# Linear attention and a SwiGLU FFN on one core: inputs laid out as (head half, 64 chunks of 9 tokens), and the work ordered anew

## The chip, the cores and the metric

One core of a Trainium2 chip. The metric is the device time of one execution in microseconds; the medians below are of two to seven executions. The span of a profile (first to last instruction) is 1.7 to 2.2 us shorter than the time of that execution. TensorE's granted clock is given where it matters. Engines: PE is TensorE, PEld its weight loads, DVE VectorE, ACT ScalarE, POOL GpSimd, SP SyncE, SPq SyncE's queue of DMA issues.

## The reference

```python
# q, k, v: (batch 8, heads 8, seq 576, head_dim 64), float32
def phi(x):
    return np.where(x > 0, x, np.exp(x) - 1.0) + 1.0
q_p, k_p = (phi(q), phi(k))
kv  = np.einsum('bhsd,bhse->bhde', k_p, v)
z   = np.sum(k_p, axis=2)
num = np.einsum('bhsd,bhde->bhse', q_p, kv)
den = np.einsum('bhsd,bhd->bhs', q_p, z)[..., None] + 1e-06
x   = (num / den)                       # -> (4608 tokens, 512)
g   = x @ w_gate                        # 512 x 1536
out = (g * sigmoid(g) * (x @ w_val)) @ w_out    # 1536 x 512
```

## The kernel before

A batch is 576 tokens. A group is 512 tokens through the FFN (12 blocks `l1`, then 4 tiles `l2`); nine groups make the 4608 tokens. The kernel before puts tokens in the partitions: 512 of a batch as 128 partitions of 4 tokens (rows of 1 KB per head), and the last 64 of two batches together as a tail tile (rows of 256 B). All tails make the ninth group. q, k and v come by one hardware queue, SyncE's; the weights by GpSimd's, which casts them to fp16 (9.44 MB of float32; its queue, q0 on the page, shows 4.72 MB). The order of issue is the program's order on each engine.

```python
def load(b, src, main, tail):
    nc.sync.dma_start(out=main[b % 2][:, :, :],
        in_=src[b][:, 0:NM, :].rearrange("h (p j) d -> p h (j d)", j=J))       # J = 4, NM = 512
    if b % 2 == 0:
        for e in range(2):
            nc.sync.dma_start(out=tail[(b // 2) % 2][TL * e:TL * e + TL, :, :], # TL = 64
                              in_=src[b + e][:, NM:S, :].rearrange("h p d -> p h d"))

def vcast(b, js):                    # ScalarE
    for j in js:
        nc.scalar.activation(out=vm[b % 2][:, j, :, 0:D], in_=v32[b % 2][:, :, D * j:D * j + D], func=AF.Copy, ...)

def mm1(b, half):                    # kv: per head pair 4 + 1 matmuls of 128 rows
    ...

for g in range(B + 1):
    ...                              # [cut: which step of batch g+1 or g+2 runs in which slot]
    for fb in range(FB):             # FB = 12
        if fb == 0 and g >= 0:
            if g + 2 < B:
                load_k(g + 2); load_q(g + 2); load_v(g + 2)
        l1(g, fb)                    # 8 matmuls, SiLU on ScalarE, product on VectorE
        run(ch[fb])                  # a step of batch g+1's attention
        ...
        if 4 <= fb < 8 and b2 < B:   # b2 = g + 2
            vcast(b2, [fb - 4])
    for t in range(4):
        l2(g, t)
        run(pa[t])                   # exp and phi of batch g+2
```

## Time and profile before

| | before |
|---|---|
| time, median (range) | 431.9 us (430.93 to 432.88) |
| span | 429.3 us |
| first matmul of the FFN | 34.9 us |
| group 0 / 1 / 2 / 3 / 4 / 5 | 76.7 / 41.7 / 45.5 / 39.1 / 46.1 / 40.4 us |
| group 6 / 7 / 8 | 36.7 / 32.0 / 31.2 us |
| after the last matmul | 4.8 us |

A group's length is the distance from its first gate matmul to that of the next, read from the timeline. The last group has nothing beside the FFN: 144 matmuls, about 0.216 us apart, make 31.2 us, so nine groups make 281 us of the span. Whatever else takes time must show as a group longer than 31.2 us or as time before the first group.

What was read first is the page's head (busy us, share of the span, count of instructions), its row of DMA queues, and for forty slices of 10.7 us the busy tenths of the DMA engines (one digit a slice) and the GB/s:

```profile
PE 332.6 (77%) x1672; PEld 154.6 (36%) x1672; DVE 240.4 (56%) x430; ACT 168.9 (39%) x271; POOL 10.5 (2%) x26
...
DMA  8899992001630069004701780046002002002004
GB/s 234 184 247 247 240 273 43 1 0 50 214 128 2 1 211 253 2 0 148 246 2 43 205 219 0 0 158 234 0 20 82 2 0 99 0 2 98 0 2 98
...
q1 hardware_dynamic: 40720, 37.75, 30.4%
```

For the first six slices the DMA engines are busy for 8 or 9 tenths of the time. The row q1 (packets, MB, share of the time of 16 engines): 0.304 x 429.3 x 16 = 2088 us of engine time for 37.75 MB.

The waits view (who, for whom: us in total, times, longest) names ScalarE waiting for v, and the timeline of ScalarE shows the longest case:

```profile
ACT vm_87 L168 <- DMA v_0_67<-in_v_dram: 42.5, 4, 22.7
...
ACT vm_88 L168 <- DMA v_1_68<-in_v_dram: 8.5, 2, 4.4
```

```profile
44.05 0.60 ACT L290 ACTIVATE sil_122<-pG_133 128x512 f16<-128x512 f32 x1 [1.13 <-PE pG_133 L287]
67.30 0.63 ACT L168 ACTIVATE vm_87<-v_0_67 128x512 f16<-128x512 f32 x1 [22.66 <-DMA v_0_67<-in_v_dram]
67.84 0.58 ACT L290 ACTIVATE sil_123<-pG_134 128x512 f16<-128x512 f32 x1
```

ScalarE runs in order. In block 4 of group 0 it reaches the v cast of batch 2, whose load is far back in the queue, and stands for 22.66 us (the bracket: idle time, and what ended it). The SiLU behind it waits too: its gate matmuls were issued by 45.36 us, and it starts at 67.84. TensorE waits with it: the next gate matmul comes at 68.47 us, after 20.14 us idle. The windows view (the stretch and its length; busy us of PE, PEld, DVE, ACT and POOL, with the number of instructions; then granted clock, DMA share, GB/s) of that stretch, under one of the first loads:

```profile
2.00:16.40 14.40, 2.97 (x20) 1.99 (x20) 6.03 (x15) 5.40 (x10) 2.17 (x9) 1.00 1.08 272
40.00:67.00 27.00, 8.33 (x39) 3.66 (x38) 2.57 (x4) 1.79 (x3) 0.00 (x0) 0.70 1.14 247
```

TensorE does 8.33 us of work in 27, at a clock of 0.70, while the DMA engines are full at 247 GB/s.

### The profile page before, as it was taken

What the parts mean: (1) busy time and instruction counts of PE and PEld (TensorE: products, weight loads), DVE (VectorE), ACT (ScalarE), POOL (GpSimd) and SP (SyncE); (2) the same over time, 40 slices, a digit from 0 to 9 for tenths busy, and PEclk for the clock granted to TensorE, in tenths of its full rate; (3) what the DMA queues carried; (4) which work ended last, traced back from release to release, by engine and by line L of the source; (5) the groups of instructions that cost most, each with busy time, mean ns of one, the idle gap of its engine ahead of it and who ended that gap; (6) DMA issues with size and microseconds to landing.
All of it is one profiled execution on the core that took longest, in us unless ns stands there. A gap on an engine that the chain in (4) does not pass through costs nothing.

```text
span 429.3 us, 4508 instructions
## 1 busy us (share of the span) xinstructions
PE 332.6 (77%) x1672; PEld 154.6 (36%) x1672; DVE 240.4 (56%) x430; ACT 168.9 (39%) x271; POOL 10.5 (2%) x26
## 2 busy tenths in 40 slices
PE   0329506386788995699879948998799999999995
PEld 0113202142334452245334523453345444444442
DVE  3583102467978663678576626786666772342431
ACT  3604006752344741564346513744365221321320
POOL 3420000000000000000000000000000000000000
PEclk9999856888899999799999996999899999999999
DMA  8899992001630069004701780046002002002004
GB/s 234 184 247 247 240 273 43 1 0 50 214 128 2 1 211 253 2 0 148 246 2 43 205 219 0 0 158 234 0 20 82 2 0 99 0 2 98 0 2 98
DMA packets 45494, 42.76 MB, mean 100 GB/s; under 512 B 13728, under 2 KB 42912, under 8 KB 45472
## 3 DMA queue, kind: packets, MB, share of 16 engines
q1 hardware_dynamic: 40720, 37.75, 30.4%
q0 software_dynamic: 4752, 4.72, 6.5%
q8 instruction: 13, 0.21, 0.2%
q14 instruction: 9, 0.07, 0.1%
HBM read 37.75 MB, written 9.44 MB: 110 GB/s over the span
## 4 chain that ended last, share of the span: by engine, by line
PE 52%; DMA 16%; SPq 15%; DVE 9%; ACT 4%; issue 3%; DVEq 0%; POOL 0%; ACTq 0%; POOLq 0%
PE pO_137 L297 11%; PE pO_138 L297 10%; SPq L102 10%; DMA v_0_67<-in_v_dram 7%; PE pG_133 L287 7%; PE pG_134 L287 7%; PE pV_135 L287 7%; PE pV_136 L287 6%; DMA v_1_68<-in_v_dram 5%; SPq L97 5%; DMA q_0_65<-in_q_dram 2%; DVE qp_81 L231 2%; DVE qp_82 L231 2%; DMA k_1_64<-in_k_dram 1%; DVE hT_121 L291 1%
## 5 line engine op out<-in xcount | busy, mean ns | idle before, releaser
L287 PEld LDWEIGHTS <-wg 128*128 128x128 f16 x432 | 42.5, 101 | 86.1 <-issue 43.9
L287 PEld LDWEIGHTS <-wv 128*128 128x128 f16 x432 | 43.5, 101 | 55.1 <-issue 7.3
L291 DVE SCALAR_TENSOR_TENSOR hT_120<-pV_136,sil_123 128x512 f16<-128x512 f32 x30 | 20.7, 689 | 61.3 <-ACT sil_123 L290 48.1
L290 ACT ACTIVATE sil_122<-pG_133 128x512 f16<-128x512 f32 x54 | 32.2, 597 | 53.2 <-PE pG_133 L287 53.1
L290 ACT ACTIVATE sil_123<-pG_134 128x512 f16<-128x512 f32 x54 | 32.1, 595 | 41.2 <-PE pG_134 L287 38.8
L287 PE MATMUL pG_134<-xT_0_112,wg 128*128 128x512 f16 x30 | 12.2, 408 | 32.9 <-ACT sil_123 L290 32.9
L291 DVE SCALAR_TENSOR_TENSOR hT_120<-pV_135,sil_122 128x512 f16<-128x512 f32 x30 | 20.7, 689 | 24.7 <-PE pV_135 L287 20.5
L297 PEld LDWEIGHTS <-hT_120 128*128 128x128 f16 x240 | 23.7, 100 | 28.4 <-issue 2.3
L303 ACT ACTIVATE osb_125<-pO_138 128x512 f32<-128x512 f32 x9 | 5.4, 597 | 65.9 <-PE pO_138 L297 65.9
L297 PE MATMUL pO_137<-wo,hT_120 128*128 128x512 f16 x120 | 29.2, 396 | 0.0
L291 DVE SCALAR_TENSOR_TENSOR hT_121<-pV_136,sil_123 128x512 f16<-128x512 f32 x24 | 16.5, 689 | 22.1 <-ACT sil_123 L290 11.6
L297 PE MATMUL pO_138<-wo,hT_120 128*128 128x512 f16 x120 | 27.5, 379 | 0.0
L297 PEld LDWEIGHTS <-hT_121 128*128 128x128 f16 x192 | 18.8, 98 | 22.6
L168 ACT ACTIVATE vm_87<-v_0_67 128x512 f16<-128x512 f32 x16 | 9.7, 625 | 42.5 <-DMA v_0_67<-in_v_dram 42.5
L291 DVE SCALAR_TENSOR_TENSOR hT_121<-pV_135,sil_122 128x512 f16<-128x512 f32 x24 | 16.5, 689 | 17.2 <-PE pV_135 L287 15.2
L297 PE MATMUL pO_137<-wo,hT_121 128*128 128x512 f16 x96 | 22.0, 379 | 0.0
L297 PE MATMUL pO_138<-wo,hT_121 128*128 128x512 f16 x96 | 22.0, 379 | 0.0
L221 DVE TENSOR_REDUCE den<-prod 128x16 f32<-128x1024 f16 x16 | 19.4, 1211 | 0.1
L301 DVE TENSOR_SCALAR osb_124<-pO_137 128x512 f32<-128x512 f32 x9 | 6.2, 691 | 17.9 <-PE pO_137 L297 17.9
L186 PE MATMUL pA_139<-vm_87,kp_79 128*128 128x129 f16 x32 | 4.6, 251 | 14.4 <-DVE kp_79 L133 13.7
L168 ACT ACTIVATE vm_88<-v_1_68 128x512 f16<-128x512 f32 x16 | 9.7, 625 | 8.5 <-DMA v_1_68<-in_v_dram 8.5
L252 PE MATMUL pA_139<-id_130,qp_81 128*128 128x128 f16 x32 | 3.8, 254 | 11.4 <-DVE qp_81 L231 11.3
(207 smaller groups left out, 663.2 us busy)
## 6 DMA issues: line engine op xcount, KB each, us to landing
k_0_63<-in_k_dram SPq DMA_DIRECT2D x4, 1024.0 KB, 6.8
v_0_67<-in_v_dram SPq DMA_DIRECT2D x4, 1024.0 KB, 9.6
q_0_65<-in_q_dram SPq DMA_DIRECT2D x4, 1024.0 KB, 9.9
k_1_64<-in_k_dram SPq DMA_DIRECT2D x4, 1024.0 KB, 7.2
q_1_66<-in_q_dram SPq DMA_DIRECT2D x4, 1024.0 KB, 9.6
v_1_68<-in_v_dram SPq DMA_DIRECT2D x4, 1024.0 KB, 11.4
out_dram<-osb_124 SPq DMA_DIRECT2D x8, 512.0 KB, 2.7
out_dram<-osb_125 SPq DMA_DIRECT2D x8, 512.0 KB, 3.3
```

What stands on the lines that cost most here:

```text
L97: nc.sync.dma_start(out=main[b % 2][:, :, :], in_=src[b][:, 0:NM, :].rearrange("h (p j) d -> p h (j d)", j=J))
L102: nc.sync.dma_start(out=tail[(b // 2) % 2][TL * e:TL * e + TL, :, :], in_=src[b + e][:, NM:S, :].rearrange("h p d -> p h d"))
L168: nc.scalar.activation(out=vm[b % 2][:, j, :, 0:D], in_=v32[b % 2][:, :, D * j:D * j + D], func=AF.Copy, bias=0.0, scale=1.0)
L186: nc.tensor.matmul(out=o, lhsT=kp[b % 2][:, j, P * hp:P * hp + P], rhs=vm[b % 2][:, j, :, :].rearrange("p h c -> p (h c)")[:, 130 * hp:130 ...
L221: nc.vector.tensor_reduce(out=den[:, cs], in_=prod[:, :, :].rearrange("p j (h d) -> p (j h) d", h=H), axis=AX.X, op=ALU.add)
L231: nc.vector.tensor_tensor(out=qv, in0=qv, in1=rden[:, H * j:H * j + H].unsqueeze(2).to_broadcast([P, H, D]), op=ALU.mult)
L287: nc.tensor.matmul(out=ps[:, :], lhsT=w[:, cc, P * fb:P * fb + P], rhs=xT[cc][g % 2][:, :], start=(cc == 0), stop=(cc == NH2 - 1))
L290: nc.scalar.activation(out=s[:, :], in_=pG[i][:, :], func=AF.Silu, bias=0.0, scale=1.0)
L291: nc.vector.scalar_tensor_tensor(out=hT[g % 2][:, fb, :], in0=pV[i][:, :], scalar=SC, in1=s[:, :], op0=ALU.mult, op1=ALU.mult)
L297: nc.tensor.matmul(out=ps[:, :], lhsT=hT[g % 2][:, fb, P * t:P * t + P], rhs=wo[:, fb, :], start=(fb == 0), stop=(fb == FB - 1))
L301: nc.vector.tensor_scalar(out=o[:, t % 2, :], in0=ps[:, :], scalar1=1.0 / SC, scalar2=None, op0=ALU.mult)
L303: nc.scalar.activation(out=o[:, t % 2, :], in_=ps[:, :], func=AF.Copy, bias=0.0, scale=1.0 / SC)
```

## The change

Its intent: no tail tiles, so every batch is handled alike, with 72 units of 64 tokens that are packed eight to a group; longer rows in the loads; and a better order at the start. Partitions are now (half of the heads, 64 chunks of 9 tokens). The kv product contracts over 64 rows, for two head halves in two row tiles of the array. Cut to its core:

```diff
-    def load(b, src, main, tail):
-        nc.sync.dma_start(out=main[b % 2][:, :, :],
-            in_=src[b][:, 0:NM, :].rearrange("h (p j) d -> p h (j d)", j=J))
-        ... (tails, cut)
+    def load(src, dst, b, lp):          # C = 64, J = 9
+        v4 = src[b].rearrange("(a l) (c j) d -> a c l (j d)", a=2, j=J)
+        for hh in range(2):
+            nc.sync.dma_start(out=dst[b % 2][C * hh:C * hh + C, 2 * lp:2 * lp + 2, :],
+                          in_=v4[hh][:, 2 * lp:2 * lp + 2, :])
...
+    def mm1(b, lp):
+        ...
+        for j in range(J):
+            for hh in range(2):
+                rows = slice(C * hh, C * hh + C)
+                nc.tensor.matmul(out=kvb[b][hh][:, 256 * lp:256 * lp + W],
+                    lhsT=kp[b % 2][rows, j, P * lp:P * lp + P],
+                    rhs=vm[b % 2][rows, j, :, :]...[:, 130 * lp:130 * lp + W],
+                    start=(j == 0), stop=(j == J - 1))
...
+    ld_k(0)
+    ld_q(0)
     ...                                                              # [cut: constants]
+    ld_v(0)
+    nc.gpsimd.tensor_copy(out=gate[:, 0:1], in_=v32[0][:, 3, 0:1])   # GpSimd waits for v
+    ld_w1(0)                              # first third of the gate and value weights
+    sp_after(wv[0:1, 0, 0:1], 2)          # SyncE waits for it
+    ld_k(1)
+    ld_q(1)
+    ld_w1(1)
+    ld_w1(2)
+    ... (second layer's weights, cut)
+    sp_after(wv[0:1, 0, DF - 512:DF - 511], 1)
+    ld_v(1)
...
-            if 4 <= fb < 8 and b2 < B:
-                vcast(b2, [fb - 4])
+        if g >= 1 and b2 < B:             # none in group 0
+            ...
+            sl[8] = sl[8] + [lambda: vcast(b2, 0)]
+            sl[9] = sl[9] + [lambda: vcast(b2, 1)]
+            if fb == 4 and b2 < B:
+                ld_k(b2)
+                ld_q(b2)
+                ld_v(b2)
```

Also in it, and cut here: batches 0, 1 and 2 take z directly from phi(k) by 64x64-tiled matmuls, so that q need not wait for v; the first four blocks of groups 0 and 1 use tanh for the sigmoid, which spares ScalarE a change of its table between exp and the FFN's activation; the second layer borrows the first layer's PSUM banks, and attention gets three banks; ScalarE copies the transposes out instead of VectorE.

## The prediction

> **What bounds it now.** Per group of 512 tokens the FFN alone needs 96 + 48 matmuls about 0.216 us apart (timeline): 31.1 us, and the last group takes just that. Nine make 280 of the 429 us span. From the chain and the windows: first FFN matmul at 34.9 us, then groups of 76.5, 41.9, 45.6, 39.1, 46.1, 40.4, 36.7, 32.0, 31.1 us, then a tail of 4.9. The group of 36.7 us waits for no load, so attention costs about 5.6 us of a group; the rest above that are stalls. ScalarE waits 42.5 + 8.5 us for v (waits view); as it runs in order, the SiLUs behind the v cast wait too, then TensorE, whose granted clock falls to 0.70 (window 40 to 67). The worst is group 0, which casts batch 2's v, landing at 67 us. Between 2 and 67 us the DMA engines are full (share about 1.1) at only 220 to 272 GB/s. Later windows of even batches (with 256-byte tail rows) show 255 to 271 GB/s at share 1.03; those of odd batches, 1 KB rows alone, 290 GB/s at 0.90, so about 320 full.
>
> **What changes.**
> 1. Rows of 2304 bytes replace 1 KB and 256 bytes: 12288 input packets for 36864.[...] I assume 290 GB/s beside the weight casts, 320 alone (estimates): a batch (3.54 MB) in 11 to 12 us for about 15.
> 2. Order: batch 0, a third of the gate/value weights, then k1 q1 beside the rest, v1 late, batch 2 after. Group 0 no longer casts batch 2's v; later casts move from blocks 4-7 to 8-9 (18 us into a group), after the loads land (13 to 16).
> 3. First FFN matmul at 22 to 25 us (v at 13, weights at 22, VectorE's chain about 24).
> 4. Group 0 stays DMA-bound: 16.5 MB (batches 0, 1, all weights) before its second layer can end: about 60 us; group 1 starts about 70 instead of 111.
> 5. kv becomes 36 row-tiled 64-row matmuls for 20 (57 ns each now): 1 to 2 us.[...] VectorE stays near 29 us per batch, ScalarE takes the transpose copies; both below 36.
>
> Almost all the gain is on the critical path: 41 us up to group 1, about 20 us of load stalls in groups 1 to 5.
>
> **Sum.** 70 + 38.5 + 37.5 + 4x36.3 + 32 + 31.1 + 4.5 = 358.8 span; +2.6 (time minus span before) gives about 362 us, range 347 to 382. Faster by over 2%: 0.97; within: 0.02; slower: 0.01.
>
> **What would show it.** First gate matmul at 22 to 26 us; group 1 at 66 to 76; in group 0 ScalarE waiting for k1/q1 and TensorE for weights; from group 2 on no ScalarE wait for v over 1 us; groups 3 to 6 of 35.5 to 37.5 us; granted clock 1.00 after 80 us.
>
> **What would make it wrong.** Half-partition DMAs or the queue's eight-deep wait could hold the rate at 250 GB/s (+10 us). Row-tiled matmuls may not overlap (+1 us a group). Three banks for attention, borrowed banks for the second layer, and the last attention matmuls at the group's end may cost 1 to 3 us per boundary. VectorE in the early groups, with extra tanh work, could delay the second layer.

## The result

| | before | after |
|---|---|---|
| time, median (range) | 431.9 us (430.93 to 432.88) | 371.63 us (371.21 to 372.05) |
| span | 429.3 us | 370.3 us |
| first matmul of the FFN | 34.9 us | 32.6 us |
| group 1 begins | 111.5 us | 80.8 us |
| groups 0 / 1 / 2 | 76.7 / 41.7 / 45.5 us | 48.1 / 41.1 / 37.0 us |
| groups 3 / 4 / 5 / 6 | 39.1 / 46.1 / 40.4 / 36.7 us | 35.6 / 36.2 / 35.6 / 35.6 us |
| groups 7 / 8 | 32.0 / 31.2 us | 32.3 / 31.2 us |
| after the last matmul | 4.8 us | 4.9 us |

The ratio is 0.8606 (95% interval 0.8545 to 0.8667). Executions over 1.5% slower than the fastest of the same kernel are left out of the means. Ratios here are those from runs of the same rounds, so not quite the ratio of the medians quoted. The granted clock was 0.999 over the span (0.936 before).

The time lies in the predicted range, but 9.6 us above the predicted 362. From group 1 on the sum agrees: predicted 288.8 us, measured 370.3 - 80.8 = 289.5. The whole miss lies before group 1, at 80.8 us for the predicted 70.

The lines of the page that answer to those shown of before:

```profile
PE 322.8 (87%) x1856; PEld 151.9 (41%) x1856; DVE 230.2 (62%) x401; ACT 180.6 (49%) x265; POOL 7.7 (2%) x16
...
GB/s 182 201 140 241 251 249 234 189 71 227 175 0 80 148 234 39 58 149 236 56 70 175 229 24 87 186 225 1 89 28 0 30 83 4 0 57 58 0 30 85
...
q1 hardware_dynamic: 19588, 37.76, 43.7%
```

Half the packets, the same bytes, and yet more engine time: 0.437 x 370.3 x 16 = 2589 us for 2088. The loads became dearer, not cheaper. The windows of the first batch's loads, of the same 27 us as above, and of a later group's loads say the same (GB/s is the last column, DMA share the one before):

```profile
2.00:18.30 16.30, 2.13 (x18) 1.77 (x18) 5.80 (x11) 7.56 (x9) 0.00 (x0) 1.00 0.94 217
40.00:67.00 27.00, 19.01 (x99) 8.52 (x97) 15.98 (x26) 11.17 (x16) 0.00 (x0) 1.00 1.12 243
159.50:173.00 13.50, 13.49 (x92) 6.09 (x92) 10.96 (x23) 6.48 (x13) 0.00 (x0) 1.00 0.83 195
```

217 GB/s in the first stretch, where the kernel before had 272. In the later group TensorE is busy 13.49 of 13.50 us: there the slower loads cost nothing. That the steady groups lose nothing is confirmed by e2 below. At the start the loads are the chain of work that ended last (start us, us, what):

```profile
2.87 5.88 DMA k_0_63<-in_k_dram
8.77 9.44 DMA v_0_67<-in_v_dram
18.87 0.87 POOL wg L116
19.74 7.56 DMA wv<-in_moe_w_val_dram
27.32 0.72 SPq L112
32.67 14.85 DMA q_1_66<-in_q_dram
```

Loads of batch 0 until 18.2 us, then the first weights, which wait for v, until 27.3, then k and q of batch 1, which wait for those weights, until 47.5. ScalarE needs k1 and q1 in blocks 0 to 3 of group 0, in order with the activations there:

```profile
ACT ek L126 <- DMA k_1_64<-in_k_dram: 4.2, 2, 2.8
...
ACT eq L126 <- DMA q_1_66<-in_q_dram: 3.3, 2, 1.8
```

The long waits for v are gone. The row-tiled kv matmuls did what they were meant to. In the timeline of TensorE the two halves start together, and a pair takes some 57 ns, so the 36 of a batch cost two stretches of about half a microsecond:

```profile
160.89 0.38 PE L273 MATMUL pV_110<-xT_1_93,wv 128*128 128x512 f16 x1
161.20 0.23 PE L166 MATMUL pX_115<-vm_75,kp_71 64*128 64x129 f16 x1
161.20 0.23 PE L166 MATMUL pX_113<-vm_75,kp_71 64*128 64x129 f16 x1
161.27 0.22 PE L166 MATMUL pX_115<-vm_75,kp_71 64*128 64x129 f16 x1
161.27 0.22 PE L166 MATMUL pX_113<-vm_75,kp_71 64*128 64x129 f16 x1
...
161.66 0.22 PE L166 MATMUL pX_115<-vm_75,kp_71 64*128 64x129 f16 x1
161.67 0.22 PE L166 MATMUL pX_113<-vm_75,kp_71 64*128 64x129 f16 x1
161.81 0.39 PE L273 MATMUL pG_109<-xT_1_87,wg 128*128 128x512 f16 x1
```

The step from the last pair to the next gate matmul is 0.14 us, where one pair follows another after 0.057; the step into the first pair is 0.31 us, where full matmuls follow after 0.216. So a change costs about 0.09 us each way; by what, no run here tells.

So two questions: where do 59 us come from, and why did the loads slow down?

### The profile page after: what moved, and what is told of

The parts are those of the page before. It is cut to its first block, busy times and chain, and to the rows that moved or that the text cites. A ratio compares the mean times of both kernels' runs of the same rounds, so it can differ in the third digit from the quotient of the medians.

```text
span 370.3 us, 4985 instructions
## 1 busy us (share of the span) xinstructions
PE 322.8 (87%) x1856; PEld 151.9 (41%) x1856; DVE 230.2 (62%) x401; ACT 180.6 (49%) x265; POOL 7.7 (2%) x16
## 4 chain that ended last, share of the span: by engine, by line
PE 67%; DMA 12%; DVE 11%; issue 4%; SPq 3%; ACT 1%; POOL 0%; DVEq 0%; ACTq 0%; POOLq 0%
PE pG_108 L273 10%; PE pG_109 L273 9%; PE pV_112 L273 7%; PE pV_110 L273 6%; PE pG_109 L292 6%; PE pV_111 L292 6%; PE pV_111 L273 6%; DMA q_1_66<-in_q_dram 6%; PE pG_108 L292 5%; PE pV_110 L292 5%; SPq L96 3%; DMA v_0_67<-in_v_dram 3%; DMA wv<-in_moe_w_val_dram 2%; DMA k_0_63<-in_k_dram 2%; DVE hT_94 L282 2%
## 5 line engine op out<-in xcount | busy, mean ns | idle before, releaser
L273 PEld LDWEIGHTS <-wg 128*128 128x128 f16 x432 | 40.5, 98 | 55.6 <-issue 12.3
L281 ACT ACTIVATE sil_96<-pG_108 128x512 f16<-128x512 f32 x50 | 29.8, 596 | 37.0 <-PE pG_108 L273 33.1
L281 ACT ACTIVATE sil_97<-pG_109 128x512 f16<-128x512 f32 x50 | 29.8, 597 | 36.2 <-PE pG_109 L273 31.5
L216 DVE TENSOR_REDUCE den<-prod 128x12 f32<-128x768 f16 x24 | 22.7, 947 | 0.3
L273 PE MATMUL pG_108<-xT_0_86,wg 128*128 128x512 f16 x30 | 11.7, 389 | 4.4 <-DVE sil_96 L278 2.5
L292 PE MATMUL pG_108<-wo,hT_94 128*128 128x512 f16 x60 | 13.8, 379 | 0.0
L292 PE MATMUL pG_109<-wo,hT_94 128*128 128x512 f16 x60 | 13.8, 379 | 0.0
L292 PE MATMUL pV_110<-wo,hT_94 128*128 128x512 f16 x60 | 13.8, 379 | 0.0
L292 PE MATMUL pV_111<-wo,hT_94 128*128 128x512 f16 x60 | 13.8, 379 | 0.0
L273 PE MATMUL pG_109<-xT_0_86,wg 128*128 128x512 f16 x30 | 11.4, 380 | 1.6 <-DVE sil_97 L278 1.6
L203 PE MATMUL pX_114<-kp_71,ones 64*64 64x256 f16 x9 | 2.1, 409 | 12.2 <-DVE kp_71 L132 12.2
L282 DVE SCALAR_TENSOR_TENSOR hT_94<-pV_111,sil_96 128x512 f16<-128x512 f32 x10 | 6.9, 690 | 9.0 <-ACT sil_96 L281 6.5
L273 PE MATMUL pG_108<-xT_0_90,wg 128*128 128x512 f16 x30 | 11.6, 387 | 0.4 <-DVE xT_0_90 L266 0.4
L273 PE MATMUL pG_108<-xT_0_92,wg 128*128 128x512 f16 x30 | 11.6, 387 | 0.0
L273 PE MATMUL pG_108<-xT_0_88,wg 128*128 128x512 f16 x30 | 11.6, 387 | 0.0
L227 DVE TENSOR_TENSOR qp_73<-qp_73,rden 128x768 f16<-128x768 f16 x12 | 11.5, 954 | 0.2
L132 DVE SCALAR_TENSOR_TENSOR kp_71<-k_0_63,ek 128x576 f16<-128x576 f32 x16 | 11.4, 755 | 0.3
L132 DVE SCALAR_TENSOR_TENSOR qp_74<-q_1_66,eq 128x576 f16<-128x576 f32 x16 | 11.4, 755 | 0.3
```

The costliest lines, as they stand in the source:

```text
L132: nc.vector.scalar_tensor_tensor(out=dst[b % 2][:, :, D * l:D * l + D], in0=src[b % 2][:, l, :].rearrange("p (j d) -> p j d", d=D), scalar ...
L203: nc.tensor.matmul(out=zps[b][hh][rows, 0:HL * D], lhsT=ones[rows, 0:C], rhs=kp[b % 2][rows, j, :], start=(j == 0), stop=(j == J - 1))
L216: nc.vector.tensor_reduce(out=den[:, 12 * c:12 * c + 12], in_=prod[:, :, :].rearrange("p j (l d) -> p (j l) d", d=D), axis=AX.X, op=ALU.add)
L227: nc.vector.tensor_tensor(out=qv, in0=qv, in1=rden[:, 12 * c:12 * c + 12].unsqueeze(2).to_broadcast([P, 12, D]), op=ALU.mult)
L273: nc.tensor.matmul(out=ps[:, :], lhsT=w[:, chan(i), P * fb:P * fb + P], rhs=xT[i][g % 2][:, :], start=(i == 0), stop=(i == 3))
L281: nc.scalar.activation(out=s[:, :], in_=pg[:, :], func=AF.Silu, bias=0.0, scale=1.0)
```

## The experiments

Theory A: a DMA to half of the partitions is slow; 64 partitions, 0 to 63 or 64 to 127, are what changed for the worse. Rival B: rows of 2304 bytes, or their order in memory, are slow. Rival C: DMAs of 295 KB are too small for SyncE's queue, in which no more than eight are outstanding in this trace (in the chain above the twelfth load, the last of v, is issued at 8.77 us, just after the fourth has landed, at 8.75; of the 122 DMAs that the trace lets one set against the eighth before them, none is issued before that one has landed). For the gain, theory D: nearly all of it is the order of the v cast, not the layout.

### e1_loads: the loads alone

A kernel of loads only, its output wrong: ten phases, each loading q, k, v of batches 0 and 1, each waiting for the one before (on SyncE's queue; not on a second one, see phases 8 and 9). The forms:

```python
half:     T[C*hh : C*hh+C, per*lp : per*lp+per, :] <- src[b].rearrange("(a l) (c j) d -> a c l (j d)", a=2, j=9)[hh][...]  # as in the change
full:     T[:, per*lp : per*lp+per, :]             <- src[b].rearrange("(l a) (c j) d -> (a c) l (j d)", a=2, j=9)[...]
full1k:   T, 128 partitions                        <- src[b][:, 0:512].rearrange("h (p j) d -> p h (j d)", j=4)            # as before
half1k:   the same rows in DMAs of 64 partitions;   fullcont: 9216 contiguous bytes for each of 128 partitions
```

> Loads alone, wrong output on purpose: ten phases, each loading q, k, v of batches 0 and 1 (7.08 MB, or 6.29 MB in the phases with 1 KB rows), each waiting for the one before. Theory A (a DMA to half of the partitions is slow): phases 1, 4 (bigger DMAs) and 6 (half, 1 KB rows) run at about 230 GB/s, the same share-corrected rate that the changed kernel shows; phases 2 and 3 (128 partitions, rows of 2304 B, 590 or 295 KB each) and 5, 7 (128 partitions, 1 KB rows; contiguous) at 290 GB/s or more; phases 8 and 9 (the two halves from two queues) in between or as fast as full. Theory B (the 2304-byte row or the order in memory is slow): phases 1 to 4, 8, 9 all at 230, only 5, 6, 7 fast. Theory C (small DMAs and the eight-deep wait): phases 1 and 3 slow, 2 and 4 fast, 8 and 9 fast. Phase 10 repeats phase 1 within 5%.

Measured, as the distance from one tensor's landing to the next (VectorE reads each as it lands), and the rate that follows from the tensor's bytes (1.180 MB, or 1.049 MB for 1 KB rows):

| phase | form | us per tensor | GB/s |
|---|---|---|---|
| 1, 10 | 64 partitions by turns, 2304 B, 295 KB | 4.9, 5.0 | 241, 234 |
| 2 | 128 partitions, 2304 B, 590 KB | 3.0 | 392 |
| 3 | 128 partitions, 2304 B, 295 KB | 3.0 | 392 |
| 4 | 64 partitions, 2304 B, 590 KB | 5.25 | 225 |
| 5 | 128 partitions, 1 KB, 1 MB | 3.0 | 350 |
| 6 | 64 partitions, 1 KB, 262 KB | 4.5 | 232 |
| 7 | 128 partitions, contiguous | 2.9, then 4.6 to 10.7 | 406, then less |
| 8 | halves from SyncE and ScalarE | 2.9, then up to 6 | none (see below) |
| 9 | halves from SyncE and GpSimd | 3.0 | none (see below) |

Theory A holds and B and C fall: row length is worth 12% (350 to 392), the size of a DMA nothing over 128 partitions (phases 2 and 3), and over 64 the bigger DMA is no faster (phase 4); the half costs nearly 40%. The bytes moved in a stretch inside each phase (windows view) agree with the table within 3% for phases 1 to 7 and 10 (242, 382, 389, 224, 352, 233, 400 and 234 GB/s).

Phases 8 and 9 give no rate for two queues. The barrier before each holds back SyncE, but not the queue that is new in the phase, so its halves could load while the phase before was still running. Of GpSimd's 14 operations, the 12 loads of phase 9 and two of its barrier, 11 stand between 202.1 and 230.6 us, in phase 8. The bytes moved were 187 GB/s from 238 to 254 us, in phase 9, where a tensor every 3.0 us would need 393; in phase 8 they were 207 GB/s from 205 to 216 us. Such early loads may also be what slows phases 7 and 8 late; that is not shown.

### e13_stripes: which partitions

The half form again, and the same DMAs with one thing changed, the partitions they write:

```diff
-                nc.sync.dma_start(out=T[i][C * hh:C * hh + C, 2 * lp:2 * lp + 2, :], in_=v4[hh][:, 2 * lp:2 * lp + 2, :])
+                nc.sync.dma_start(out=T[i][hh:128:2, 2 * lp:2 * lp + 2, :], in_=v4[hh][:, 2 * lp:2 * lp + 2, :])
```

> Loads alone again, wrong output on purpose, seven phases of 7.08 MB: 1 half partitions by turns (as in the change), 2 the same DMAs (64 partitions, 295 KB, 2304-byte rows, one queue) to every second partition instead, 3 all 128 partitions, 4 the halves one after the other, 5 halves from two queues, 6 as 2, 7 as 1. [...]the stripes [...]run like the full DMA: 3.0 to 3.3 us per tensor of 1.18 MB, while phases 1, 4 and 7 stay at 4.9 to 5.3. Rival: a DMA to 64 partitions is slow as such[...]: stripes at 4.9 too. Phase 5 started at 2.9 and slowed to over 5 at its end the first time; I expect 3 to 5.

VectorE's timeline, the first read of k, v, q, k in phase 1 (halves by turns) and of v, q, k, v in phase 2 (stripes); the idle time in brackets is the wait for the load:

```profile
9.63 0.33 DVE L52 COPY gate<-t 64x1 f32<-64x1 f32 x2 [0.84 <-DMA t<-in_k_dram]
...
14.60 0.33 DVE L52 COPY gate<-t 64x1 f32<-64x1 f32 x2 [0.84 <-DMA t<-in_v_dram]
...
19.57 0.32 DVE L52 COPY gate<-t 64x1 f32<-64x1 f32 x2 [0.84 <-DMA t<-in_q_dram]
...
24.54 0.33 DVE L52 COPY gate<-t 64x1 f32<-64x1 f32 x2 [0.83 <-DMA t<-in_k_dram]
...
47.26 0.33 DVE L52 COPY gate<-t 64x1 f32<-64x1 f32 x2 [0.45 <-DMA t<-in_v_dram]
...
50.25 0.32 DVE L52 COPY gate<-t 64x1 f32<-64x1 f32 x2 [0.42 <-DMA t<-in_q_dram]
...
53.28 0.33 DVE L52 COPY gate<-t 64x1 f32<-64x1 f32 x2 [0.45 <-DMA t<-in_k_dram]
...
56.27 0.33 DVE L52 COPY gate<-t 64x1 f32<-64x1 f32 x2 [0.42 <-DMA t<-in_v_dram]
```

Halves: 4.97 us per tensor (237 GB/s). Stripes: 3.00 (393), as fast as all 128 partitions (3.01 in phase 3), and again 3.01 in phase 6. Halves from two queues landed every 2.83 us, to the end; that gives no rate either, as the barrier before phase 5 does not hold back ScalarE. The halves one after the other missed my 4.9 to 5.3: 7.5 us on average (158 GB/s), 5.4 at first and up to 10.1 later. In phase 4 of e1, with bigger DMAs in the same order, it was 5.25 throughout. ScalarE's halves of phase 5 may have loaded beside the later tensors; that is not shown.

So it is not the number of partitions in a DMA but which ones: with 64 partitions in each DMA, the same bytes, rows and queue, every second partition gave 393 GB/s, and partitions 0 to 63 and 64 to 127 by turns gave 237 (225 in phase 4 of e1, with bigger DMAs). Why, no run here shows.

### e2_full128: the same in the kernel

Heads go to the partition halves by parity, not by half, so one DMA fills 128 partitions; the rows of the gate and value weights follow, and the result stays right.

```diff
-        v4 = src[b].rearrange("(a l) (c j) d -> a c l (j d)", a=2, j=J)
-        for hh in range(2):
-            nc.sync.dma_start(out=dst[b % 2][C * hh:C * hh + C, 2 * lp:2 * lp + 2, :], in_=v4[hh][:, 2 * lp:2 * lp + 2, :])
+        v3 = src[b].rearrange("(l a) (c j) d -> (a c) l (j d)", a=2, j=J)
+        nc.sync.dma_start(out=dst[b % 2][:, 2 * lp:2 * lp + 2, :], in_=v3[:, 2 * lp:2 * lp + 2, :])
 ... the two waits for the weights now read the half that comes last [cut]; weights:
+            rows = src[:, 512 * i:512 * i + 512].rearrange("(lp l2 hh e) f -> l2 lp e hh f", lp=2, l2=2, hh=2)
+            for l2 in range(2):
+                for lp in range(2):
+                    nc.gpsimd.dma_start(out=dst[64 * l2:64 * l2 + 64, 2 * lp:2 * lp + 2, 512 * i:512 * i + 512], in_=rows[l2][lp])
 ... chan(i): return i
```

> The changed kernel with heads split over the partition halves by parity, so that one DMA fills all 128 partitions (six DMAs of 590 KB a batch for twelve of 295); the rows of the gate and value weights are permuted for it, in DMAs of 64 partitions. The result stays right. Theory A: batch 0's v lands at 13 to 15 us for 18.2, loads in the steady groups take 11 to 13 us, group 1 starts at 72 to 77 us for 81, total 362 to 367 us for 371.6 (the halved weights may eat part). Theories B: no change of rate, total 370 to 373. Theory C: like A here (bigger DMAs), so the loads-only run must tell these two apart.

364.5 us; ratio to before 0.8452 (0.8412 to 0.8492), clear of the change's 0.8545 to 0.8667. v of batch 0 lands at 12.9 us for 18.2, group 1 begins at 73.1 for 80.8, and groups 3 to 6 stay at 35.61. The row of the queue, and the chain's start:

```profile
q1 hardware_dynamic: 18820, 37.76, 33.1%
```

```profile
3.27 9.62 DMA v<-in_v_dram
```

Engine time is 0.331 x 362.0 x 16 = 1917 us, below both kernels. The first FFN matmul, however, comes only at 29.6 us, 16.7 us after v and 7.0 after the first weights: not the loads but the chain of batch 0's attention now bounds the start.

What the faster loads bring is an earlier q of batch 1. ScalarE's timeline has the last exp of it, in the change and then in e2:

```profile
47.60 1.16 ACT L126 ACTIVATE eq<-q_1_66 128x1152 f16<-128x1152 f32 x1 [1.47 <-DMA q_1_66<-in_q_dram]
39.94 1.16 ACT L127 ACTIVATE eq<-q 128x1152 f16<-128x1152 f32 x1 [1.24 <-DMA q<-in_q_dram]
```

It begins 7.7 us earlier, and so does group 1. From its begin to group 1 it is 33.2 us in both: the rest of group 0, with batch 1's attention in it. Eight of the ten profiles of the changed kernel and its variants show 33.2 or 33.3 us there (e3 34.8, e5 35.2).

### e3_halfweights: are the halved weights dear?

e2 loads the weights in halves. Alone, in the changed kernel:

```diff
     ... [cut: the two waits for the weights read partition 64, the half that comes last]
+            rows = src[:, 512 * i:512 * i + 512].rearrange("(c p) f -> p c f", p=P)
+            for l2 in range(2):
+                nc.gpsimd.dma_start(out=dst[64 * l2:64 * l2 + 64, :, 512 * i:512 * i + 512], in_=rows[64 * l2:64 * l2 + 64])
```

> The changed kernel with each gate and value weight load split into two DMAs of 64 partitions, nothing else. It bounds what the permuted weights cost in the 128-partition version. If half-partition DMAs on the GpSimd queue suffer like those of the SyncE queue (240 for 392 GB/s alone), the first third of the weights lands 1 to 3 us later than 27.3 us and group 1 starts 0 to 3 us later than 80.8: total 371 to 375 us. If they do not suffer: 370.5 to 372.5.

373.27 us, ratio 0.8627 (0.8578 to 0.8677): not to be told from the change. Group 1 begins at 83.5 us, but the unedited kernel showed 80.8 and 81.1, and e5 below, whose loads are untouched, 83.0. A cost of up to some 2 us is possible and not shown.

### e4_twoqueues: both halves in flight

```diff
-            nc.sync.dma_start(
+            (nc.gpsimd if hh else nc.sync).dma_start(
```

> The changed kernel with the loads of the second partition half issued from the GpSimd queue, so that both halves are in flight at once. Theory A[...]:[...] v of batch 0 lands at 14 to 16 us, total 364 to 369. If the cost belongs to each half-partition DMA whatever else is in flight, no gain: 370 to 374. The second-half loads of batch 1 then stand ahead of the later weights in the same queue, which may shift a few us within group 0.

364.81 us, ratio 0.8453: as good as e2, with no other layout. Group 1 begins at 74.0. But v lands at 16.8 us, later than expected, and the windows show that the loads did not become faster as in e2:

```profile
2.00:18.00 16.00, 2.25 (x22) 2.02 (x24) 6.91 (x15) 7.82 (x9) 4.41 (x9) 1.00 0.86 221
...
40.00:60.00 20.00, 18.03 (x97) 8.28 (x94) 14.37 (x25) 8.10 (x13) 4.05 (x7) 1.00 1.17 244
```

221 and 244 GB/s, as in the change (221 from 2 to 18 us, 243 from 40 to 67). What moved is the order: SyncE's wait for the first weights does not hold the halves on GpSimd's queue, so those of k1 and q1 are issued from 19.2 us on for 28.1. The last exp of q1 begins at 40.9 us for 47.6, and group 1 33.2 us after it. So e4 does not show that two queues restore the rate in the kernel, and for loads alone e1 and e13 cannot tell.

### e7_before_vlate: the order of the v cast alone

The kernel before, with only the v cast of batch g+2 moved:

```diff
-            if 4 <= fb < 8 and b2 < B:
-                vcast(b2, [fb - 4])
-                if fb == 7:
+            if 8 <= fb < 12 and 0 < g and b2 < B:
+                vcast(b2, [fb - 8])
+                if fb == 11:
                     vcast_tail(b2)
 ... at the end of group 0:
+            vcast(2, [0, 1, 2, 3])
+            vcast_tail(2)
```

> The kernel before, with the v cast of the batch after next moved: in groups 1 to 5 from blocks 4-7 to 8-11, in group 0 from blocks 4-7 to its end. It tests how much of the gain is the order alone. My theory (ScalarE, in order, held by v): group 0 shrinks from 76.5 us to 55-65, groups 1 to 5 lose most of the 20 us above 37, total 395 to 410 us for 431.9. Rival (the loads themselves set the pace, whoever waits for them): total within 3% of 431.9.

385.4 us, ratio 0.8927 (0.8895 to 0.8958): better than my 395 to 410. Group 0 takes 57.3 us for 76.7, groups 2 to 6 take 36.1 to 36.7. ScalarE's wait for v falls from 51.0 us to this:

```profile
ACT vm L168 <- DMA v<-in_v_dram: 3.0, 2, 2.0
```

Theory D holds for three quarters, not for nearly all: of 59.0 us of span that the change saves, 429.3 - 384.1 = 45.2 can be had by moving one cast. Of the 13.8 us beyond that, group 1 beginning earlier (91.9 to 80.8) is 11.1, and groups 1 to 6 (224.1 us to 221.1) 3.0; the rest loses 0.3.

### e5_rowserial: do the row tiles pay?

```diff
-        for j in range(J):
-            for hh in range(2):
+        for hh in range(2):
+            for j in range(J):
```

> The changed kernel with the 36 kv matmuls of a batch issued half after half (18 of rows 0 to 63, then 18 of rows 64 to 127, in two calls of 9 + 9) instead of alternating. Theory: the alternating pairs run side by side (57 ns a pair in the trace, 1.03 us a batch); in series a batch takes about 36 x 57 ns = 2.05 us, so groups 3 to 6, which TensorE bounds, grow from 35.6 to 36.6 us and the total by 5 to 8 us, to 376 to 380. Rival: the row halves cost nothing extra (the array is not the limit[...]): 371 to 373.

376.7 us, ratio 0.8701 (0.8654 to 0.8747; this overlaps the change's 0.8545 to 0.8667 a little, so the groups say more than the time). The 18 kv matmuls of a call take 0.92 us to the next gate matmul for 0.61 in the change, so running side by side saves 0.3 us per call, 0.6 per batch, where I expected 1.0: one after another they come some 50 ns apart, not 57.

```profile
164.39 0.98 PE L166 MATMUL pX<-vm,kp 64*128 64x129 f16 x18
165.31 1.04 PE L273 MATMUL pG<-xT,wg 128*128 128x512 f16 x4
```

Groups 3 to 6 take 36.0 to 36.2 us for 35.6, and groups 1 to 6 together 223.6 for 221.1 (220.6 in e12): 2.5 to 3 us. The rest of the difference in span, 2.2 us, lies before group 1 (83.0 for 80.8). It is not the loads, as the last exp of q1 begins at 47.8 us (48.0 in e12), but why this edit should cost so much there stays open.

### e8_nogate: k1 and q1 without waiting for the first weights (on e2)

```diff
-    sp_after(wv[64:65, 2, 0:1], 2)
```

> The 128-partition version without the wait that holds k and q of batch 1 back until the first third of the weights has landed. The DMA engines were only 0.80 busy from 2 to 18 us and moved 185 GB/s from 18 to 27 us. If the arrival of k1/q1 still holds ScalarE in group 0 (it waited until 37 and 40 us for q1), group 0 shrinks from 43.5 to 38-41 us and the total goes from 364.5 to 359-362. Rival: the first weights then land later and the first gate matmul slips from 29.6 to over 31 us: no gain, 363 to 366.

361.54 us, ratio 0.837 (0.831 to 0.8429). The interval overlaps that of e2 (0.8412 to 0.8492), so the gain is read from the profile: first FFN matmul 29.6, unchanged; group 0 41.5 us for 43.5 (I had put 38 to 41); group 1 begins at 71.1.

### e9_shift: the steady order one group sooner (on e8)

```diff
-        if g < 2:
+        if g < 1:
             sl, w = early(b1)
-        elif g == 2:
+        elif g == 1:
             sl, w = late(b1)
 ...
+        if g == 0:
+            pre[2] = [lambda: exp_k(2, 0), lambda: exp_k(2, 1)]
+            pre[3] = [lambda: exp_q(2, 0), lambda: exp_q(2, 1)]   # and vcast(2) after block 0 of group 1
 ... [cut: phi of k and tanh in the early blocks shifted in the same way]
```

> The version before this one (128 partitions, no wait) with the steady order of work begun one group sooner: the exps of batch 2 in group 0's second layer, group 1 as group 2 was, group 2 as group 3. Expected if the loads now arrive in time: group 1 37 us for 41, group 2 35.6 for 37.0, total 353 to 358 us. If k2/q2/v2 are still late, ScalarE waits for them at the end of group 0 and the gain is lost: 359 to 364.

357.88 us, ratio 0.8268 (0.8227 to 0.8309). Group 1 takes 38.0 us for 41.1, group 2 35.8 for 37.0.

### e10_expq: batch 0's q ahead of the direct z (on e9)

```diff
-    z_direct(0)
     for lp in range(2):
         exp_q(0, lp)
         phi_q(0, lp)
+    z_direct(0)
```

> The fastest version so far (128 partitions, no wait, steady order one group sooner), with the exps and phi of batch 0's q emitted ahead of the direct z, so that ScalarE no longer holds them behind the z copies (4.3 us idle there, VectorE 4.2 us idle after it). Expected: the first gate matmul moves from 29.9 to 25.5-27 us, and as the loads are now early enough, most of it reaches the end: 353.5 to 356.5 us for 357.9. Rival: group 0 is still held by k1/q1 or the weights: group 1 unmoved at 71.5, total 357 to 359.

354.38 us, ratio 0.8168 (0.8121 to 0.8214), the result right: the fastest version found. Its ratio over the change's is 0.8168 / 0.8606, so about 5% less time than the change. First FFN matmul at 25.9 us, group 1 at 68.1 for 71.5.

### e11_after_expq and e12_after_again: the same in the changed kernel, and the changed kernel itself

e11 has e10's edit on the change; e12 is the change unedited.

> The same reordering in the changed kernel itself, with its half-partition loads. Theory: group 0 is bound by its loads there, so the first gate matmul may come 1.5 to 4 us sooner (from 32.6), but group 1 stays at 80 to 83 us and the total at 370 to 373. Rival (VectorE's chain of batch 0 is on the critical path there too): total 367 to 369.

> The changed kernel again, unedited, beside the two: 370 to 373 us, and group 1 at 80 to 83 us. It shows how far group 0 differs from one profile to the next; two variants of it that should not differ much showed 83.0 and 83.5.

e11: 372.09 us, ratio 0.8588 (0.8528 to 0.8649). e12: 372.76, 0.86 (0.8546 to 0.8654). The first FFN matmul moved from 32.9 to 28.8 us, and group 1 from 81.1 to 80.2 only. In the change the last exp of q1 waits for its load (1.5 us idle before it; it begins at 46.9 us in e11, 48.0 in e12), so a faster chain before it buys nothing clear of the noise; in e9 and e10 the load is there, the exp begins at 38.2 and 34.8, and the same edit buys 3.5 us. The loads come early there for two reasons, all 128 partitions (e2) and no wait for the weights (e8).

## Why the prediction was right, and where it missed

- **The direction and most of the size: right, and for the reason given.** ScalarE held in order by the v cast was the main loss; e7 shows 45.2 us of it by moving the cast alone. The split was less right: 41 us were to be gained up to group 1, and 30.7 were.
- **Groups 1 to 8: right.** The sum was 288.8, measured 289.5. Groups 3 to 6 were to take 35.5 to 37.5 us and took 35.6 to 36.2; ScalarE has no long wait for v any more; the clock is full (0.999). Group 1 was 2.6 us longer than I put it, groups 3 to 6 together 2.2 us shorter; that these two cancel is luck.
- **Step 1, "I assume 290 GB/s beside the weight casts, 320 alone (estimates): a batch (3.54 MB) in 11 to 12 us for about 15": wrong, in sign.** I counted packets and rows, which are worth 12% (e1), and not which partitions a DMA writes, which costs 40%. Batch 0 took until 18.2 us at 217 GB/s where the kernel before had 272. I did name it under what could make me wrong ("Half-partition DMAs ... could hold the rate at 250 GB/s (+10 us)"), and it came about so. Step 4, group 1 at about 70 us, was the term that was mis-sized by it: it measured 80.8. With the loads mended and little else, e2 begins group 1 at 73.1, so 7.7 of the 10.8 us are the loads. The path in step 4 was wrong too. It counted the bytes until batch 1 and all weights have landed, "about 60 us", and even at the slow rate the last of them landed at 60.0. What group 1 waits for is the chain behind q1: it begins 33.2 us after the last exp of q1, here (47.6) as in e2 (39.9). The time stayed in the range because the range left 20 us above 362, while two of the signs named beforehand failed: the first gate matmul at 22 to 26 us (32.6) and group 1 at 66 to 76 (80.8).
- **Step 3, "First FFN matmul at 22 to 25 us (v at 13, weights at 22, VectorE's chain about 24)": wrong twice.** v landed at 18.2 for 13. And even with v at 12.9 and the weights at 22.6 (e2) the matmul comes at 29.6: I had summed VectorE's work and missed that ScalarE holds exp(q) behind the z copies. e10 moves it to 25.9. In the changed kernel itself the same edit moves it from 32.9 to 28.8, but group 1 by only 0.9, as q1 lands late (e11).
- **TensorE waiting for weights in group 0** was expected and is not seen: it waits for ScalarE and VectorE, which wait for k1 and q1.
- **Step 5, the kv matmuls: right.** About 1.1 us a batch with the tiles overlapping, against 1 to 2 predicted. Their worth is smaller than thought, 0.6 us a batch (e5).

Left open: the spread of group 0 between profiles of nearly equal kernels (80.2 to 83.5 us for the begin of group 1), the late slowing of two phases of e1 and of phase 4 of e13, what two queues do to the rate of loads alone, and why the partitions that a DMA writes set its rate.

## What to carry to other kernels

An engine that runs in order must not be given, early in a group, an operation on data whose load is last in the queue; where its place in the program is free, moving one cast can be worth more than a new layout (here 45.2 of 59.0 us, e7). Loads that go by turns to partitions 0 to 63 and 64 to 127 on one queue lost nearly 40% of the rate in a kernel of loads alone (234 to 241 GB/s for 392): lay the data out so that one DMA covers all 128 partitions (shown in the kernel by e2) or every second one (393 GB/s, shown for loads alone). Two queues helped in the kernel by the order, not by the rate (221 and 244 GB/s, e4); for loads alone no run here tells. Do not size a start-up by its bytes only: ask which load the longest chain hangs on (here q of batch 1, 33 us before group 1). And when a start-up bound by loads gets its loads mended, look at once for the next chain behind it: here one reordering was worth nothing clear of the noise before and 3.5 us after.
